# The kernel transform of an S4D convolution: first stage in three float16 products, normalisation and copies on ScalarE

## The chip, the cores and the metric

The kernel runs on one core of a Trainium2 chip. A core has five engines that run their own instruction streams: TensorE (PE, matrix products into PSUM), VectorE (DVE), ScalarE (ACT), GpSimd (POOL) and SyncE (SP, which here only issues transfers). Each engine works through its instructions in order and waits on semaphores of the others. The metric is the device time of one execution in microseconds (us), lower is better; the median of the runs is compared.

## The reference

Four layers are applied one after the other to `x` (2048 positions, 640 channels), each to the layer-normalised `x` and added to it: attention (32 heads of 20), an S4D convolution, the same attention and the same convolution again.

```python
x = x + _A_ref(_layernorm(x), A_wqkv, A_wo)
x = x + _B_ref(_layernorm(x), B_log_A_real, B_A_imag, B_C_real, B_C_imag, B_log_dt, B_D_skip)
x = x + _A_ref(_layernorm(x), A_wqkv, A_wo)
x = x + _B_ref(_layernorm(x), B_log_A_real, ...)

def _B_ref(u, ...):                     # the convolution
    P = jnp.exp((A * dt[:, None])[:, :, None] * pos[None, None, :])
    K = 2.0 * jnp.einsum("dn,dnl->dl", C, P).real        # 640 kernels of length 2048
    Kf = jnp.fft.rfft(K, 2 * L)
    Uf = jnp.fft.rfft(u_t, 2 * L)
    y = jnp.fft.irfft(Uf * Kf[None, :, :], 2 * L)[:, :, :L]
    return y + u * D_skip[None, None, :]
```

The kernels `K` do not depend on `x`, so they and their transforms are computed once and serve both convolutions.

## The kernel before

**The order of the program.** First a prologue: layer norm, the first projections and the tables of powers from which `K` is built (`kgen`). Then attention of the first layer, during which `kgen` makes `K` piece by piece in the gaps of VectorE and TensorE and writes it to `kd` in memory, 32 channels at a time. Then `out_proj` (the attention's output projection), into which `ktransform` is woven; then the convolution `ssm`; then attention, `out_proj` and `ssm` of the second pair, without `kgen` and `ktransform`. A scheduler fixes the order of instructions on each engine when the program is built. In attention a planner with costs of its own decides what goes between two exponentials.

**`out_proj`** runs over 16 slices `s` of the positions (128 each). Per slice it does 30 products of 320 columns: `L1099` with the low part `ol` of the attention's output, `L1105` with its high part `oh`, into two banks `po` of PSUM. VectorE adds `po` to `x` and takes the statistics of the rows (`BN_STATS`, `BN_AGGR`, then `va`, `lt`, `rs`). `ln_u` makes the normalised rows `u` on VectorE, ScalarE rounds them to float16 (`uh`), and GpSimd, or for the last slice VectorE, takes the rest (`ul`). The first convolution needs `uh` and `ul` of all slices. In the first pair the low part `ol` has one buffer, in the second two.

**`ktransform`** runs over five units of 128 channels. A unit
- loads 1 MB of `kd` into `kl` (one buffer) and adds the skip weight to its first column,
- turns it round in 16 transposes `pkt` (`L1054`), four to a bank; VectorE and ScalarE take turns in copying the banks to `ktr`,
- does the first stage, 32 float32 products `pkx` of 128 columns (`L1062`) with the cosine and sine matrix `e1` of 2 MB; the eight banks are copied to `kx` by ScalarE and VectorE in turn,
- goes eight times through `q`: four transposes (`L1071`) into a bank, a copy to `kxt` on ScalarE, a float32 product `pkf` of 512 columns (`L1079`), two shuffles of it to the two halves of `kn` on VectorE, and a sign on one half by ScalarE. Two rounds of `q` fill a pair `kn`, and two transfers of 512 KB write it to `kha` and `khb`. The pair has one buffer.

In the profile a float32 product counts as two matmul records. The tiles `pkt`, `pkx`, `pkf` and `po` have two banks each. The profile shows tile names without their trailing digits; names that then coincide stand with a number in the listings of order below.

**`ssm`** begins with `stage1` (`L1164`): the same transform of the normalised rows, already as three float16 products with a high and a low part of the matrix (`e1s`), twelve products of 128 columns to a bank. ScalarE copies the bank to the high part of `x1`, VectorE takes the low part (both read `x` in the profile: `x<-psx`). `stage2a` (`L1174`) transposes these.

Of the kernel before, what the change touches and what calls it, by code (L numbers as in the profile page):

```python
# [21 lines left out]
P = 128  # L22
L = 2048
D = 640
NI = L // P
NCT = D // P
# [58 lines left out]
def mha_s4d_kernel(ctx, tc, x_in, wqkv, wo, lar, aim, cr, ci, ldt, dsk,  # L85
                   c_e1, c_eb, c_f2, c_fa, c_sel, c_lv, c_id, c_sg, c_e16, c_f16, c_id16, out, parts="asas", general=None):
# [25 lines left out]
    kd = dram.tile([D, L], F32, name="kd")  # L112
# [17 lines left out]
    ve.memset(hpi, math.pi / 2)  # L130
    flag = cp.tile([P, 2], F32, name="flag")
    warm = cp.tile([P, 1], F32, name="warm")
    ve.memset(flag, 0.0)
    with tc.tile_pool(name="op", bufs=1) as op:
        oneh = op.tile([1, L], F16, name="oneh")
# [46 lines left out]
    def kgen():  # L182
# [8 lines left out]
        for n, a in (("lar", lar), ("aim", aim), ("cr", cr), ("ci", ci)):  # L191
            ld[n] = (klp if n in ("lar", "aim") else kp).tile([P, D], F32, name="k_" + n)
            if n in ("lar", "aim"):
                sy.dma_start(ld[n], a)
        dt = klp.tile([P, D], F32, name="k_dt")
        d5 = klp.tile([P, D // P], F32, name="k_d5")
        ge.dma_start(d5, ldt.rearrange("o (p c) -> (o p) c", c=D // P))
# [144 lines left out]
        for r in range(2):  # L342
            ve.memset(tab[:, r, :, 0:24].rearrange("p d (g k) -> p d g k", k=8)[:, :, :, 0:1], 1.0 - r)
        yield from expand(0, kpw[0], tab, dif)
        load_powers(2)
        yield
        for k in range(NE):
# [663 lines left out]
            return oh, ol  # L1011
        return split, lambda: o.append(load(0))

    def ln_u(x, i0, n, mvrs, uh, ul, pool):
        mv, rs = mvrs
        for i in range(n):
            s = i0 + i
            u = pool.tile([P, D], F32, name="u")
            ve.tensor_scalar(u, x[:, s, :], mv[:, i, 0:1], rs[:, i:i + 1], ALU.subtract, ALU.mult)
            se.copy(uh[:, s, :], u)  # L1020
            (ve if s == NI - 1 else ge).tensor_sub(ul[:, s, :], u, uh[:, s, :])  # L1021

# [4 lines left out]
    def by_channel(x1, i2):  # L1027
        return x1[:, :, i2].rearrange("p g (s c) -> p s g c", c=4)

    def ktransform():  # L1030

        c = ExitStack()
        c1 = c.enter_context(tc.tile_pool(name="f1", bufs=1))
        c2 = c.enter_context(tc.tile_pool(name="f2", bufs=2))
        e1 = c1.tile([P, NI, 2, P], F32, name="e1")
        sy.dma_start(e1, c_e1.rearrange("p (i r k) -> p i r k", i=NI, r=2))
        f2 = c1.tile([P, P], F32, name="f2")
        sy.dma_start(f2, c_f2)
        sgn = c1.tile([P, 1], F32, name="sgn")
        sy.dma_start(sgn, c_sg)  # L1040

        skip = c1.tile([P, NCT], F32, name="skip")
        sy.dma_start(skip, dsk)

        def unit_load(b):
            kl = c1.tile([P, L], F32, name="kl")
            sy.dma_start(kl, kd[b * P:b * P + P, :])
            ve.tensor_add(kl[:, 0:1], kl[:, 0:1], skip[:, b:b + 1])
            kt = c1.tile([P, NI, P], F32, name="ktr")
            klv = kl.rearrange("d (p i) -> d i p", i=NI)  # L1050
            for i4 in range(4):
                pt = pst("T", [P, 4, P], F32, tag="T", name="pkt")
                for i in range(4):
                    te.transpose(pt[:, i, :], klv[:, 4 * i4 + i, :], ident)  # L1054
                (se.copy if i4 % 2 else ve.tensor_copy)(kt[:, 4 * i4:4 * i4 + 4, :], pt)
                yield
            x1 = c1.tile([P, 32, NI // 2, 16], F32, name="kx1")
            for i2 in range(NI // 2):
                ps = pst("X", [P, 2, 2, P], F32, tag="X", name="pkx")
                for r in range(2):  # L1060
                    for i in range(2):
                        te.matmul(ps[:, r, i, :], e1[:, 2 * i2 + i, r, :], kt[:, 2 * i2 + i, :],  # L1062
                                  start=True, stop=True)
                (ve.tensor_copy if i2 % 2 else se.copy)(by_channel(x1, i2), ps.rearrange("p r i (g c) -> p (r i) g c", c=4))
                yield
            prev = None
            for q in range(9):
                if q < 8:
                    pt = pst("T", [P, 4, P], F32, tag="T", name="pkt")
                    for g in range(4):  # L1070
                        te.transpose(pt[:, g, :], x1[:, 4 * q + g].rearrange("p i s -> p (i s)"), ident)  # L1071
                    xt = c2.tile([P, 512], F32, name="kxt")
                    se.copy(xt, pt.rearrange("p g k -> p (g k)"))
                if prev is not None:
                    g0 = b * 32 + 4 * (q - 1)
                    if q % 2:
                        kn = [c1.tile([P, 2, 512], F32, name=f"kn{s}") for s in range(2)]
                    px = pst("F", [P, 512], F32, tag="F", name="pkf")
                    te.matmul(px, f2, prev, start=True, stop=True)  # L1079
# [268 lines left out]
    def seq(x, general):  # L1348

        stats = None  # L1350
        for n in range(0, len(parts), 2):
            with ExitStack() as c:
                if general:
                    if stats is not None:
                        xpools.pop().__exit__(None, None, None)
                    attention_general(x)
                else:
                    x, wc, *tail = attention(x, stats)
                psum(c, X=2)
                c3 = ExitStack()  # L1360
                if n == 0 and not general:
                    psum(c3, M=2, T=2, F=2)
                else:
                    psum(c3, M=4)
                up = c.enter_context(tc.tile_pool(name="up", bufs=1))
                uh = up.tile([P, NI, D], F16, name="uh")
                ul = up.tile([P, NI, D], F16, name="ul")
                consts = ssm_consts(c)
                with ExitStack() as c2:
                    up2 = c2.enter_context(tc.tile_pool(name="up2", bufs=2))  # L1370

                    def ln(i0, m):
                        ln_u(x, i0, m, ln_stats(lambda i: x[:, i0 + i, :], m), uh, ul, up2)
                    if general:
                        for i0 in range(0, NI, LG):
                            ln(i0, LG)
                    else:
                        if n == 0:
                            filler[:] = ktransform(), 0.0, False
# [91 lines left out]
```

## Time and profile before

| | us |
|---|---|
| median of 3 runs | 2705.94 |
| lowest and highest | 2704.41, 2708.41 |
| the profiled execution's own time | 2710.14 |
| its span from first to last instruction | 2708.3 |
| TensorE busy in the span | 2532.1 (93%) |
| ScalarE busy | 2336.7 (86%) |
| VectorE busy | 1478.1 (55%) |
| GpSimd busy | 853.2 (32%) |
| `out_proj` of the first pair, first to last of its products | 1104.4 to 1285.5 |

The profile is of one execution. Its rows give a start, a duration and, in brackets, the idle time of the engine just before the instruction and what ended it. Matmuls overlap: a row's duration is the time through the array, and the spacing of starts is what a product costs in a stream. "PEclk" is the TensorE clock that was granted, 1.00 being full speed. The listings of groups give, after the bar, the busy time of all instructions of the group, the mean duration in ns, and the idle time before them with the engine and tile that ended it.

### The profile page before, as it was taken

Reading aid. Unit: us, or ns where it says so; the run is one execution under the profiler, and the core shown is the slowest. Engines: PE = TensorE matmul, PEld = TensorE weight load, DVE = VectorE, ACT = ScalarE, POOL = GpSimd, SP = SyncE. Lnnn points to the kernel's source line nnn. Section 1 sums busy time; section 2 is a strip of 40 time slices with the busy share of each in tenths; the row PEclk is TensorE's granted clock in tenths of the full one; section 3 lists DMA queues with packets and bytes.
Section 4 is the critical chain, followed back from the end, with each engine's and each line's share of the span. In section 5 each row is a group of like instructions: output and inputs, shape, how many; then the busy total and the mean of one; then the engine's idle time right before and its main releaser. Section 6 shows DMA issues by size and latency. Waiting matters only on the chain.

```text
span 2708.3 us, 115632 instructions
## 1 busy us (share of the span) xinstructions
PE 2532.1 (93%) x50944; PEld 1443.4 (53%) x50944; DVE 1478.1 (55%) x3292; ACT 2336.7 (86%) x2762; POOL 853.2 (32%) x1282
## 2 busy tenths in 40 slices
PE   6899999999999998899999999999999998888998
PEld 3445444444444433777896544454454443335888
DVE  7677877777856993567776423232233220003865
ACT  7899989999999999555655899999999999997464
POOL 1132323233332334300671122222223223222376
PEclk9999999999999999999999999999999999999999
DMA  6523222322221224454642111211121112112365
GB/s 205 182 59 78 63 77 57 81 60 70 62 54 49 56 67 140 148 193 189 193 152 67 48 53 50 53 56 46 43 64 41 51 37 60 41 38 81 112 190 162
DMA packets 183152, 238.55 MB, mean 88 GB/s; under 512 B 42736, under 2 KB 128240, under 8 KB 180848
## 3 DMA queue, kind: packets, MB, share of 16 engines
q1 hardware_dynamic: 146304, 184.48, 21.3%
q0 software_dynamic: 36336, 46.59, 7.6%
q8 instruction: 402, 6.59, 1.0%
q14 instruction: 110, 0.90, 0.1%
HBM read 154.90 MB, written 76.03 MB: 85 GB/s over the span
## 4 chain that ended last, share of the span: by engine, by line
ACT 50%; PE 29%; issue 9%; DVE 7%; DMA 4%; POOL 0%; SPq 0%; ACTq 0%; DVEq 0%; POOLq 0%
ACT pt L77 49%; PE pa L842 5%; PE S L825 3%; PE psv L1199 3%; PE po L1105 3%; PE psy L1209 2%; PE m L578 2%; PE psx L1187 2%; PE psx L1164 2%; PE po L1099 1%; PE pst L1174 1%; PE pkf L1079 1%; DMA kop<-ks 1%; PE pq L731 1%; PE pkx L1062 1%
## 5 line engine op out<-in xcount | busy, mean ns | idle before, releaser
L77 ACT ACTIVATE pt<-S 128x1024 f32<-128x1024 f32 x2048 | 1922.5, 1037 | 40.3 <-PE S L825 30.8
L842 PE MATMUL pa<-pt,V 64*32 64x512 f32 x16384 | 1104.2, 591 | 1.0 <-DVE oc L77 0.6
L825 PE MATMUL S<-qop,kop 61*32 61x512 f16 x16384 | 884.7, 381 | 118.0 <-ACT pt L77 102.5
L825 PEld LDWEIGHTS <-kop 61*32 61x32 f16 x16384 | 374.6, 90 | 777.5 <-issue 653.5
L77 POOL DMA_DIRECT2D dn<-oc x256 | 125.7, 497 | 732.9 <-DVE oc L77 696.3
L842 PEld LDWEIGHTS pa<-pt,V 64*32 64x32 f32 x16384 | 316.5, 106 | 72.4 <-issue 8.9
L77 DVE TENSOR_SCALAR qc<-m 128x512 f32<-128x512 f32 (+1 forms) x68 | 46.8, 689 | 313.7 <-PE m L578 313.7
L77 DVE COPY oc<-pa 128x512 f32<-128x512 f32 x64 | 44.2, 690 | 305.3 <-PE pa L842 297.6
L77 POOL DMA_DIRECT2D db<-dn x256 | 129.5, 512 | 131.3 <-DMA dn<-dr 128.0
L578 PE MATMUL m<-xh,wh 64*32 64x512 f16 x2560 | 148.7, 380 | 1.6 <-DVE qc L77 1.6
L578 PE MATMUL m<-xh,wl 64*32 64x512 f16 x2560 | 149.0, 379 | 0.0
L578 PE MATMUL m<-xl,wh 64*32 64x512 f16 x2560 | 146.9, 378 | 0.0
L77 POOL DMA_DIRECT2D ot<-oc x256 | 129.8, 515 | 11.3 <-issue 5.2
L578 PEld LDWEIGHTS <-wh 64*32 64x32 f16 x5120 | 93.1, 94 | 74.8 <-issue 33.0
L1192 POOL TENSOR_TENSOR t<-t,kb 128x512 f32<-128x512 f32 x80 | 101.8, 1273 | 70.7 <-DVE t L77 69.7
L77 ACT COPY xt<-pst 128x1024 f16<-128x1024 f16 x80 | 81.6, 1023 | 46.7 <-PE pst L1174 46.6
L77 POOL DMA_DIRECT2D dn<-dr x64 | 35.7, 558 | 244.9 <-DVE dr L77 235.2
L77 DVE TENSOR_SCALAR V<-m 128x160 f32<-128x160 f32 x64 | 20.7, 324 | 160.0 <-PE m L544 160.0
L77 DVE TENSOR_TENSOR kb<-ktab 128x512 f32<-128x512 f32 x160 | 107.8, 693 | 0.0
L544 PEld LDWEIGHTS <-xh 128*128 128x128 f16 x960 | 79.6, 98 | 48.0 <-issue 32.8
L1021 POOL TENSOR_TENSOR ul<-u,uh 128x640 f16<-128x640 f32 x30 | 46.2, 1557 | 177.1 <-ACT uh L77 177.1
L1193 POOL TENSOR_TENSOR t<-t,t 128x512 f32<-128x512 f32 x78 | 99.1, 1271 | 7.3 <-DVE t L77 1.3
(269 smaller groups left out, 3952.2 us busy)
## 6 DMA issues: line engine op xcount, KB each, us to landing
ka<-kha SPq DMA_DIRECT2D x80, 256.0 KB
kb<-khb SPq DMA_DIRECT2D x80, 256.0 KB
db<-dn POOLq DMA_DIRECT2D x256, 64.0 KB, 2.8
kpw<-wd POOLq DMA_DIRECT2D x60, 192.0 KB, 5.1
qop<-qs SPq DMA_DIRECT2D x256, 40.0 KB
kop<-ks SPq DMA_DIRECT2D x128, 80.0 KB
ot<-oc POOLq DMA_DIRECT2D x256, 40.0 KB, 2.7
otl<-ot SPq DMA_DIRECT2D x32, 320.0 KB
```

The lines of the kernel that those rows point to most:

```text
L77: made = f(out, *a, **k)
L544: chain(te.matmul(ps[:, :n], a_[:, ct, sl], m[:, ct, :], start=(k == 0), stop=(k == 14)))
L578: chain(te.matmul(ps[r][32 * t:32 * t + 32, :], a_[rows, ct, 32 * u:32 * u + 32], m[rows, ct, 512 * v:512 * v + 512], start=(k == 0), stop ...
L825: chain(te.matmul(S[32 * t:32 * t + 32, 512 * r:512 * r + 512], kt_[rows, kc + 32 * t:kc + 32 * t + 32], qt[rows, :], start=True, stop=Tru ...
L842: chain(te.matmul(pa[r][32 * j:32 * j + 32, :], V[rows, kt, VP * h:VP * h + 32], pts[j // 2][rows, 512 * (j % 2):512 * (j % 2) + 512], sta ...
L1105: te.matmul(pos[hf], oh[:, ct, :], m[:, ct, 320 * hf:320 * hf + 320], start=False, stop=(ct == NCT - 1 and m is wol))
L1164: te.matmul(ps[:, r, i, :], e1[:, e, s, r, :], m[:, s, bs], start=(n == 0), stop=(n == 2))
L1187: te.matmul(px, f2[:, f, :], xt[:, k, :], start=(n == 0), stop=(n == 2))
L1192: ge.tensor_mul(t2, t2, kb)
L1193: (ge if g0 else ve).tensor_add(t1, t1, t2)
L1199: te.matmul(pv[:, g].rearrange("p r i c -> p (r i c)"), t1[:, g * P:g * P + P], fa, start=True, stop=True)
L1209: te.matmul(py[:, i, :], eb[:, 4 * i4 + i, r, :], v[:, r, 4 * i4 + i].rearrange("p g c -> p (g c)"), start=(r == 0), stop=(r == 1))
```

## The change

The first stage of `ktransform` is now computed as `stage1` computes it, in three float16 products with `e1s`, which `ssm` has loaded anyway; the float32 matrix `e1` and its load of 2 MB are gone. So that `K` fits float16, it is scaled by a power of two that is found from the largest values of the inputs (`kbig`, `kmost`, `bound`); the scale is undone in the copy to `kxt`.

```diff
+            ve.reduce_max(big[:, n:n + 1], t, axis=AX.X, apply_absolute_value=True)   # three of them, in kgen
+        ge.partition_all_reduce(most, big, P, bass.bass_isa.ReduceOp.max)
+        slow.append((1, bound))                                     # bound(): seven operations on one column
...
-    def ln_u(x, i0, n, mvrs, uh, ul, pool):
+    def ln_u(x, i0, n, mvrs, uh, ul, pool, on_act):
+        if on_act:
+            nb = sm.tile([P, n], F32, name="nb1")
+            ve.scalar_tensor_tensor(nb, mv[:, :, 0], -1.0, rs, ALU.mult, ALU.mult)
...
+            if on_act:
+                se.activation(u, x[:, s, :], AF.Identity, scale=rs[:, i:i + 1], bias=nb[:, i:i + 1])
+            else:
+                ve.tensor_scalar(u, x[:, s, :], mv[:, i, 0:1], rs[:, i:i + 1], ALU.subtract, ALU.mult)
...
-        e1 = c1.tile([P, NI, 2, P], F32, name="e1")
-        sy.dma_start(e1, c_e1.rearrange("p (i r k) -> p i r k", i=NI, r=2))
...
+        def load(b):
+            kl = c2.tile([P, L], F32, name="kl")
+            sy.dma_start(kl, kd[b * P:b * P + P, :])
+            return kl
+        kls = [load(0)]
         def unit_load(b):
-            kl = c1.tile([P, L], F32, name="kl")
-            sy.dma_start(kl, kd[b * P:b * P + P, :])
+            kl = kls.pop()
+            if b + 1 < NCT:
+                kls.append(load(b + 1))
...
-                (se.copy if i4 % 2 else ve.tensor_copy)(kt[:, 4 * i4:4 * i4 + 4, :], pt)
+                se.activation(hi[:, s4, :], pt, AF.Copy, scale=ksc[:, 0:1])
+                ve.scalar_tensor_tensor(lo[:, s4, :], pt, ksc[:, 0:1], hi[:, s4, :], ALU.mult, ALU.subtract)
...
-                for r in range(2):
-                    for i in range(2):
-                        te.matmul(ps[:, r, i, :], e1[:, 2 * i2 + i, r, :], kt[:, 2 * i2 + i, :],
-                                  start=True, stop=True)
-                (ve.tensor_copy if i2 % 2 else se.copy)(by_channel(x1, i2), ...)
+                for i in range(2):
+                    s = 2 * i2 + i
+                    for r in range(2):
+                        for n, (e, m) in enumerate(((0, hi), (0, lo), (1, hi))):
+                            te.matmul(ps[:, r, i, :], e1[:, e, s, r, :], m[:, s, :], start=(n == 0), stop=(n == 2))
+                (ve.tensor_copy if i2 % 4 == 1 else se.copy)(by_channel(x1, i2), ...)
...
-                    se.copy(xt, pt.rearrange("p g k -> p (g k)"))
+                    se.activation(xt, pt.rearrange("p g k -> p (g k)"), AF.Copy, scale=ksc[:, 1:2])
...
-                        kn = [c1.tile([P, 2, 512], F32, name=f"kn{s}") for s in range(2)]
+                        kn = [c2.tile([P, 2, 512], F32, name=f"kn{s}") for s in range(2)]
```

`c1` has one buffer per tile and `c2` two, so `kl` and `kn` now have two. `on_act` holds for the first pair only: there the 16 normalised rows `u` are made by ScalarE.

The scheduler has laid out the surroundings anew, in the prologue, in the first `out_proj` and for a few transfers between; attention keeps its order, and nothing is moved from the first `stage2a` on. Three places matter. In the changed kernel the lines are further down: `L1054` is `L1085`, `L1062` is `L1097`, `L1071` is `L1105` (which before was a line of `out_proj`), `L1079` is `L1113`, and `out_proj`'s two lines are `L1133` and `L1139`.

TensorE in the rounds of `q` of the first unit; before:

```order
L1079 MATMUL pkf<-kxt,f_26611 128x512
L1071 MATMUL pkt<-ident,kx_26645 128x128 x8
L1099 MATMUL po<-woh,ol 128x320 x2
L1071 MATMUL pkt<-ident,kx_26645 128x128 x4
L1105 MATMUL po<-woh,oh 128x320
```

and of the change:

```order
L1113 MATMUL pkf<-kxt,f_26627 128x512
L1105 MATMUL pkt<-ident,kx_26668 128x128 x4
L1085 MATMUL pkt<-ident,kl 128x128 x4
L1133 MATMUL po<-woh,ol 128x320 x3
L1085 MATMUL pkt<-ident,kl 128x128 x2
```

Before, after the fourth `pkf` of a unit, a block of 16 to 20 products of `out_proj` stood ahead of the next `pkf`. Now the first six `pkf` of a unit follow one another with only their transposes between, and the transposes of the next unit begin before the last two. The first transposes of `ktransform` stand behind 184 products of `out_proj` (before: 240 of the 480), and 170 are left when its last `pkf` is through (before: 25).

VectorE at the end of `out_proj`, from the statistics of the last slice; before:

```order
L77 BN_AGGR mv<-st 128x2
L77 TENSOR_SCALAR lt<-lt 128x1
L77 TENSOR_SCALAR va<-mv 128x1
L77 TENSOR_TENSOR rs<-rs,lt 128x1
L77 TENSOR_SCALAR u<-x,mv,rs 128x640
L77 RECIPROCAL rs<-lt 128x1
```

with the first `x_28307<-psx_28308,x_28306` eight rows further, behind the last `ul<-u,uh`; and of the change:

```order
L77 BN_AGGR mv<-st 128x2
L77 TENSOR_SCALAR va<-mv 128x1
L77 TENSOR_TENSOR x_28684<-psx_28685,x_28683 128x4x32x4
L77 RECIPROCAL rs<-lt 128x1
L77 TENSOR_TENSOR lt<-rs 128x1
L77 TENSOR_TENSOR lt<-lt,va 128x1
L77 TENSOR_TENSOR x_28684<-psx_28700,x_28683 128x4x32x4
```

Seven of the first eight low parts of `stage1` now stand ahead of the last `ul`; before, all of them stood behind it.

SyncE's queue near the end of attention, of the change:

```order
L77 DMA wot<-in_wo 128x640 x5
L77 DMA x<-in_x_in 128x2560
L77 DMA kl<-kd 128x2048
L77 DMA qop_107<-qs 40x1x512
L77 DMA qop_107<-qs 20x512
```

The first load of `kl` has come into attention, ahead of the queries `qop` of its last block of 512 (the row `kl` is new there, the others are as before). It waits for the writes of `kd`.

More of the change, by code (lines that the diff above doesn't have):

```diff
@@ L132, in mha_s4d_kernel @@
     warm = cp.tile([P, 1], F32, name="warm")
+    ksc = cp.tile([P, 2], F32, name="ksc")
     ve.memset(flag, 0.0)
@@ L194, in kgen @@
                 sy.dma_start(ld[n], a)
+        big = kp.tile([P, 3], F32, name="kbig")
+        most = kp.tile([P, 3], F32, name="kmost")
+        skip = kp.tile([P, NCT], F32, name="kskip")
+        sy.dma_start(skip, dsk)
         dt = klp.tile([P, D], F32, name="k_dt")
@@ L344, in kgen, with bound @@
         yield from expand(0, kpw[0], tab, dif)
+        for n, t in enumerate((ld["cr"], ld["ci"], skip)):
+            ve.reduce_max(big[:, n:n + 1], t, axis=AX.X, apply_absolute_value=True)
+        ge.partition_all_reduce(most, big, P, bass.bass_isa.ReduceOp.max)
+        def bound():
+            b = big[:, 0:1]
+            bits = b.bitcast(mybir.dt.int32)
+            ve.tensor_add(b, most[:, 0:1], most[:, 1:2])
+            ve.tensor_scalar(b, b, float(P), 1e-30, ALU.mult, ALU.max)
+            ve.tensor_add(b, b, most[:, 2:3])
+            ve.tensor_single_scalar(bits, bits, 0x7F800000, ALU.bitwise_and)
+            ve.reciprocal(ksc[:, 0:1], b)
+            ve.tensor_scalar_mul(ksc[:, 0:1], ksc[:, 0:1], 2.0 ** 14)
+            ve.tensor_scalar_mul(ksc[:, 1:2], b, 2.0 ** -14)
+        slow.append((1, bound))
         load_powers(2)
@@ L1018, in ln_u @@
             u = pool.tile([P, D], F32, name="u")
-            ve.tensor_scalar(u, x[:, s, :], mv[:, i, 0:1], rs[:, i:i + 1], ALU.subtract, ALU.mult)
+            if on_act:
+                se.activation(u, x[:, s, :], AF.Identity, scale=rs[:, i:i + 1], bias=nb[:, i:i + 1])
+            else:
+                ve.tensor_scalar(u, x[:, s, :], mv[:, i, 0:1], rs[:, i:i + 1], ALU.subtract, ALU.mult)
             se.copy(uh[:, s, :], u)
@@ L1028, in by_channel, with ktransform @@
         return x1[:, :, i2].rearrange("p g (s c) -> p s g c", c=4)
-    def ktransform():
+    def ktransform(e1):
         c = ExitStack()
@@ L1043, in ktransform @@
         sy.dma_start(skip, dsk)
+        def load(b):
[3 more added lines that the diff above has]
+        kls = [load(0)]
         def unit_load(b):
-            kl = c1.tile([P, L], F32, name="kl")
-            sy.dma_start(kl, kd[b * P:b * P + P, :])
+            kl = kls.pop()
+            if b + 1 < NCT:
+                kls.append(load(b + 1))
             ve.tensor_add(kl[:, 0:1], kl[:, 0:1], skip[:, b:b + 1])
-            kt = c1.tile([P, NI, P], F32, name="ktr")
+            hi, lo = (c1.tile([P, NI, P], F16, name=f"ktr{n}") for n in "hl")
             klv = kl.rearrange("d (p i) -> d i p", i=NI)
@@ L1054, in unit_load @@
                     te.transpose(pt[:, i, :], klv[:, 4 * i4 + i, :], ident)
-                (se.copy if i4 % 2 else ve.tensor_copy)(kt[:, 4 * i4:4 * i4 + 4, :], pt)
+                s4 = slice(4 * i4, 4 * i4 + 4)
+                se.activation(hi[:, s4, :], pt, AF.Copy, scale=ksc[:, 0:1])
+                ve.scalar_tensor_tensor(lo[:, s4, :], pt, ksc[:, 0:1], hi[:, s4, :], ALU.mult, ALU.subtract)
                 yield
@@ L1059, in unit_load @@
                 ps = pst("X", [P, 2, 2, P], F32, tag="X", name="pkx")
-                for r in range(2):
-                    for i in range(2):
-                        te.matmul(ps[:, r, i, :], e1[:, 2 * i2 + i, r, :], kt[:, 2 * i2 + i, :],
-                                  start=True, stop=True)
-                (ve.tensor_copy if i2 % 2 else se.copy)(by_channel(x1, i2), ps.rearrange("p r i (g c) -> p (r i) g c", c=4))
+                for i in range(2):
[3 more added lines that the diff above has]
+                            te.matmul(ps[:, r, i, :], e1[:, e, s, r, :], m[:, s, :], start=(n == 0), stop=(n == 2))
+                (ve.tensor_copy if i2 % 4 == 1 else se.copy)(by_channel(x1, i2), ps.rearrange("p r i (g c) -> p (r i) g c", c=4))
                 yield
@@ L1372, in ln @@
                     def ln(i0, m):
-                        ln_u(x, i0, m, ln_stats(lambda i: x[:, i0 + i, :], m), uh, ul, up2)
+                        ln_u(x, i0, m, ln_stats(lambda i: x[:, i0 + i, :], m), uh, ul, up2, n == 0 and not general)
                     if general:
@@ L1378, in seq @@
                         if n == 0:
-                            filler[:] = ktransform(), 0.0, False
+                            filler[:] = ktransform(consts[0]), 0.0, False
                         out_proj(x, *tail, ln)
```

## The prediction

> **What bounds the kernel now.** I read busy time by stretch first. Columns: from:to, length, then busy time (and instructions) of PE, PE's weight loads, DVE, ACT, POOL, the granted clock, DMA share and GB/s.
>
> ```profile
> core 0: us, PE busy (x) PEld busy (x) DVE busy (x) ACT busy (x) POOL busy (x), PEclk, DMA share, GB/s
> 130.00:600.00 470.00, 456.60 (x12484) 227.78 (x12479) 367.13 (x758) 453.78 (x483) 147.52 (x252) 1.00 0.27 67
> ...
> 80.00:100.00 20.00, 17.53 (x91) 8.09 (x89) 15.02 (x30) 19.41 (x30) 0.00 (x0) 1.00 0.70 262
> ...
> 1104.00:1294.00 190.00, 179.74 (x1178) 150.49 (x1171) 139.91 (x369) 90.18 (x154) 30.90 (x33) 0.99 0.54 196
> 1290.00:1300.00 10.00, 6.03 (x71) 5.86 (x70) 7.61 (x10) 5.18 (x10) 1.29 (x1) 0.66 0.85 310
> ```
>
> In attention ACT works 453.78 of 470 us: what the change adds there on VectorE and GpSimd has to delay ACT before it costs anything. In the prologue ACT is full too (19.41 of 20). In the first `out_proj`, where the change lies, PE is the full engine: 179.74 of 190 us, against 139.91 on DVE and 90.18 on ACT. So next comes the order of time on PE (start, duration, line, tile, records; in brackets idle time and what ended it).
>
> ```profile
> 1104.37 1.73 PE L1099 MATMUL po<-woh,ol 128*128 128x320 f32 x10
> ...
> 1144.76 1.14 PE L1054 MATMUL pkt<-ident,kl 128*128 128x128 f32 x8 [1.47 <-issue]
> 1146.23 1.17 PE L1054 MATMUL pkt<-ident,kl 128*128 128x128 f32 x8 [0.33 <-DVE ktr L77]
> 1147.23 7.84 PE L1062 MATMUL pkx<-ktr,e 128*128 128x128 f32 x64
> 1154.83 1.13 PE L1099 MATMUL po<-woh,ol 128*128 128x320 f32 x6
> ...
> 1158.65 1.02 PE L1079 MATMUL pkf<-kxt,f 128*128 128x512 f32 x2
> 1159.51 0.60 PE L1071 MATMUL pkt<-ident,kx 128*128 128x128 f32 x4
> 1159.95 1.08 PE L1079 MATMUL pkf<-kxt,f 128*128 128x512 f32 x2
> ...
> 1285.47 0.23 PE L1164 MATMUL psx<-uh,e1s 128*128 128x128 f16 x1
> ...
> 2480.63 1.70 PE L1099 MATMUL po<-woh,ol 128*128 128x320 f32 x10 [1.65 <-DVE oc L77]
> 2550.95 0.31 PE L1105 MATMUL po<-wol,oh 128*128 128x320 f32 x1
> ```
>
> The second pair's `out_proj` has the same 480 products alone: 2480.63 to 2550.95 and one more product, 70.5 us. In the first pair it takes 1104.37 to 1285.47, 181.1 us. Its parts: `out_proj` 70.5; 40 rounds of `q` of 1.30 (1158.65 to 1159.95), 52.0; 80 transposes of 0.125 (eight from 1146.23 to 1147.23), 10.0; five first stages of 7.60 (1147.23 to 1154.83), 38.0. Sum 170.5, so PE loses about 10.6 us to waits. The stage is bound by PE's own work, and work taken from PE is worth its time.
>
> **The change part by part.** *First stage.* The 64 records of a unit (320 in all) cost 7.60/64 = 119 ns each. The 96 float16 products that replace them have the shape, type and matrix of `stage1`; twelve of these, undisturbed, stand between these rows:
>
> ```profile
> 1348.68 0.22 PE L1164 MATMUL psx<-uh,e1s 128*128 128x128 f16 x1
> ...
> 1349.35 1.11 PE L1199 MATMUL psv<-fa,t 128*128 128x128 f32 x8
> ...
> L1164 PEld LDWEIGHTS <-e1s x960: 95/98/148, 1285.5 to 2662.2; 128*128 128x128 f16 x192
> ```
>
> 0.67 us for twelve, 56 ns each; 480 cost 26.8 us instead of 38.0: **-11.2 us**. A weight load takes 98 ns by the third row (minimum/median/maximum), but loads overlap there, since products start every 56 ns. Were this hidden part lost, 480 x 98 = 47.0 us would stand in place of 38.0, a loss of 9.0; these are the two ends, and I take the first, as the rows are of the same instruction. The Trainium skill, "TensorE: Matmul & The Clock Gate", section "Back-to-back issue gap", gives about 81 ns per product of 128 columns for a sustained stream of weight loads and products, and calls some 56 ns the figure of a single gap. By it the stage would cost an estimated 480 x 81 = 38.9 us, and the exchange would gain nothing; this trace has 56 ns in a stream and disagrees.
>
> *Copies around it.* Groups of this stage (busy, mean ns of one):
>
> ```profile
> L77 DVE STREAM_SHUFFLE kn<-pkf 128x512 f32<-128x512 f32 x80 | 54.8, 737 | 0.1
> L77 DVE COPY kx<-pkx 128x512 f32<-128x512 f32 x20 | 13.8, 688 | 8.1 <-PE pkx L1062 8.0
> L77 ACT COPY kx<-pkx 128x512 f32<-128x512 f32 x20 | 11.7, 584 | 17.4 <-PE pkx L1062 17.3
> L77 DVE COPY ktr<-pkt 128x512 f32<-128x512 f32 x10 | 6.8, 683 | 1.2 <-PE pkt L1054 1.2
> L77 DVE TENSOR_SCALAR u<-x,mv,rs 128x640 f32<-128x640 f32 x16 | 11.2, 725 | 0.7
> L77 DVE TENSOR_TENSOR lt<-rs 128x2 f32<-128x2 f32 x7 | 1.1, 155 | 0.1
> ...
> L77 ACT ACTIVATE xr<-xr,nb,rs 128x640 f32<-128x640 f32 x16 | 14.0, 926 | 2.2 <-DVE nb L77 2.0
> ```
>
> DVE loses the 16 `u` (11.2), 10 `ktr` (6.8) and 10 of 20 `kx` (6.9): 24.9 us. It gains 20 low parts `lo`, an operation that the trace does not show; between the shuffle's 0.737 and the `ktr` copy's 0.683 us I take 0.69, the plain copy of the same bank: 13.8 us. With nine `nb` of 0.155 that is -9.7 net: 139.9 falls to 130. ACT gains 10 `hi` and 10 `kx` at 0.584 and 16 `u` at 0.926 (the `xr` row is this very operation): 5.8 + 5.8 + 14.8 = 26.4; 90.2 becomes 117 of some 178 us, still two thirds full. Neither becomes the bound over the stage, so I cost the copies at nothing; PE's work covers them. Locally: twelve products fill a bank in 0.67 us, and two banks are emptied by ACT in 0.584 or DVE in 0.688; with 0.1 us of handover that is (0.67 + 0.69 + 0.1)/2 = 0.73 per bank at worst against 0.67, 40 x 0.06 = 2.4 us if it held throughout.
>
> *Waits inside the stage, and the order.* Wait groups name this one:
>
> ```profile
> DVE kn L77 <- DMA kha<-kn: 8.7, 5, 2.2
> ```
>
> DVE stands 8.7 us, five times, because the single pair `kn` is still being written out; the second pair removes that, and the early load of `kl` the 1.47 us ahead of 1144.76. At the same time the rounds of `q` now follow one another with little `out_proj` between. Each round needs two shuffles, 2 x 0.737 = 1.47 us of DVE, and PE needs 1.30: 40 x 0.17 = 6.8 us lost if DVE did nothing else and PE had nothing to slip in. So the sum of waits, 10.6 before, may fall by 8 or rise by 7. The two have the same size, and I take 0. Also the 2 MB load of `e1` is gone; PE's own rows show no wait for a transfer there but the 1.47, so it is worth nothing.
>
> *The end of the stage.* Between PE's last `po` and the first transposes of `stage2a`:
>
> ```profile
> 1293.91 0.27 PE L1164 MATMUL psx<-uh,e1s 128*128 128x128 f16 x1 [5.04 <-DVE x L77]
> ...
> 1299.34 0.40 PE L1174 MATMUL pst<-id,x 128*128 128x128 f16 x4
> ...
> 1290.01 1.63 DVE L77 TENSOR_SCALAR u<-x,mv,rs 128x640 f32<-128x640 f32 x1
> 1292.43 0.82 DVE L77 TENSOR_TENSOR ul<-u,uh 128x640 f16<-128x640 f32 x1 [0.79 <-ACT uh L77]
> 1293.17 2.48 DVE L77 TENSOR_TENSOR x<-psx,x 128x512 f16<-128x512 f32 x4
> ...
> 2561.68 0.61 PE L1174 MATMUL pst<-id,x 128*128 128x128 f16 x8 [0.37 <-ACT x L77]
> ```
>
> First pair: 1285.47 to 1299.34, 13.9 us. PE waits 5.04 us for a low part `x<-psx` that is queued on DVE behind the last `u` and `ul`, and then runs at a lower clock (0.66 granted in 1290 to 1300). In the second pair, whose `x<-psx` do not stand behind the last `ul`, the same takes 2551.10 to 2561.68, 10.6 us. The new order lets the low parts go ahead as in the second pair: at most -3.3. But the last `u` costs 0.926 + 0.155 on ACT, and ACT also copies `x`: at worst the new chain is 0.9 longer than before. I take **-2.0**.
>
> *Prologue.*
>
> ```profile
> L77 ACT ACT_TABLE_LOAD x18 | 23.1, 1283 | 1.8 <-PEq L1460 0.7 <-PE S L825 0.7
> ```
>
> ACT's new order has one table load more ahead of attention, 1.283 us on a full engine: **+1.3**. The reordering may leave it covered (0) or put up to two more loads' time on the chain (+4).
>
> *Attention.* VectorE takes three reductions and some seven one-column operations (0.155 each), GpSimd one maximum over partitions; all are under ACT's cover, cost 0. The `kl` load now stands in SP's queue ahead of the last `qop`, and waits for the last write of `kd`:
>
> ```profile
> 1041.63 1.10 SPq L77 DMA_DIRECT2D qop<-qs  x2
> ...
> 1047.28 0.25 SPq L77 DMA_DIRECT2D qop<-qm  x1
> ...
> L77 POOL DMA_DIRECT2D kd<-ko x1: 957/957/957, 1047.3 to 1047.3; - x1
> ...
> DMA to landing us min/median/max: 8.6/8.6/8.6
> ...
> 1099.69 0.41 PE L825 MATMUL S<-qop,kop 61*32 61x512 f16 x8 [0.35 <-ACT pt L77]
> ...
> 1101.53 0.41 PE L825 MATMUL S<-qop,kop 61*32 61x512 f16 x8 [0.35 <-ACT pt L77]
> ```
>
> `kd` lands at 1047.3 + 8.6 = 1056; the twelve `qop` loads, which took 5.7 us to issue (1041.63 to 1047.28), then end near 1062. They serve the last 512 columns, 16 pairs of products spaced 1.84 us (1099.69 to 1101.53), so from about 1101.5 - 16 x 1.84 = 1072 on. Some 10 us of margin: cost 0; if a landing took twice as long, PE and then ACT would stall up to 5.
>
> Sum: -11.2 - 2.0 + 1.3 = -11.9. The profiled execution becomes 2710.14 - 11.9 = 2698.2; it lies 4.2 above the median of the runs, so the median becomes 2705.94 - 11.9 = **2694.0**, faster by 0.44%.
>
> **The rivals.** *Denser:* the second `kn` pair, the early `kl` and a DVE with 10 us less work take out most of PE's waits. For it: 8.7 of DVE's idle time has this one cause. Against it: PE mostly had `out_proj` products to run meanwhile. 2694.0 - 7 = 2687. *Given back:* the packed rounds of `q` run at DVE's pace. For it: 1.47 over 1.30, and `lo` falls to the same engine. Against it: the next unit's first stage and `out_proj` fill gaps. 2694.0 + 6.8 = 2700.8. *Weight loads not hidden (slower):* each of the new first stages switches matrix and operand within one stream, and if loads did not overlap there, 98 ns would set the pace: 2705.94 + 9.0 - 2.0 + 1.3 = 2714.2. It decides from 79 ns per product (38.0/480) on. Against it stand the 56 ns of `stage1`, which switches in the same way. It is also the side on which the 81 ns of the Trainium skill lie. *Cover gone:* the load of `kl` blocks SP's queue beyond 1072, and the prologue costs its +4: 2694.0 + 5 + 2.7 = 2701.7. That the change does less than it says is excluded for the main term: 96 products a unit and no load of `e1` stand in the new order.
>
> **How the numbers follow.** Forecast 0.56, denser 0.14, given back 0.16, weight loads 0.08, cover gone 0.06. About 0.2%, 5.4 us, is what a measurement of this kernel can tell from no change: faster means below 2700.5. That holds the forecast (its own range is 2688 to 2701), denser, and the smaller part of given back: 0.73. Same: the rest of given back and most of cover gone, with a rim of the forecast, 0.17. Slower: the weight loads and some of the last, 0.10. The range 2685 to 2706 leaves out about 0.05 below and 0.12 above.
>
> **What would show it.** Right: the new `pkx` rows start every 56 ns, 5.4 us per unit; first `po` to first `psx` takes about 170 us; the last `po` to the first `pst` takes 11 to 12; no PE wait above 1 us for `qop` near 1072. Given back shows as PE's waits for DVE `kn` ahead of `pkf`, 7 us or more; denser as a stage of 162 us or less with no DVE wait for `kha`; the weight loads as `pkx` spacings near 98 ns. The forecast is wrong if the stage's work falls by 11 us while its length falls by less than 5.

## The result, and the profile after

| | before | after |
|---|---|---|
| median, us | 2705.94 (5 runs, 2704.41 to 2708.41) | 2693.66 (5 runs, 2692.22 to 2694.99) |
| ratio to before | | 0.9954, 95% interval [0.9939, 0.9968] |
| own time of the profiled execution | 2710.14 | 2693.68 |
| attention's first exponential | 116.75 | 115.36 |
| first `po` to first `psx` (the stage) | 181.1 | 170.6 |
| from the product behind the last `po` to first `pst` (its end) | 13.9 | 11.3 |
| first `po` to first `pst` | 195.0 | 181.9 |

The change gains 12.3 us; 11.9 were forecast. The two profiled executions differ by 16.5 us, since that of before lies 4.2 above its median; 13.1 of the 16.5 are in the last line of the table, which is therefore the line to follow.

First the busy time by stretch, for the changed kernel (columns as in the prediction):

```profile
core 0: us, PE busy (x) PEld busy (x) DVE busy (x) ACT busy (x) POOL busy (x), PEclk, DMA share, GB/s
80.00:100.00 20.00, 17.59 (x89) 7.92 (x87) 14.97 (x31) 17.76 (x29) 0.12 (x1) 0.98 0.67 247
130.00:600.00 470.00, 455.44 (x12482) 229.11 (x12489) 372.97 (x777) 453.22 (x483) 148.75 (x254) 1.00 0.26 67
1102.00:1292.00 190.00, 182.20 (x1484) 150.74 (x1479) 143.53 (x378) 126.22 (x202) 34.23 (x35) 1.00 0.52 188
1273.00:1284.00 11.00, 8.09 (x127) 7.22 (x126) 10.21 (x24) 8.10 (x15) 2.06 (x2) 1.00 0.47 145
...
1102.00:1273.00 171.00, 167.74 (x1288) 138.75 (x1283) 127.57 (x346) 113.07 (x181) 29.68 (x32) 1.00 0.50 184
```

Attention is as it was. In the stage itself (the last row) PE is busy 167.74 of 171 us, DVE 127.57, ACT 113.07: PE is still the full engine. At the end (1273 to 1284) the granted clock is 1.00, where 0.66 was granted in 1290 to 1300 before.

The order of time on PE for the changed kernel, from the first `po` over one run of the new first stage to the first `pst`:

```profile
1102.33 1.73 PE L1133 MATMUL po<-woh,ol 128*128 128x320 f32 x10
...
1141.20 0.22 PE L1097 MATMUL pkx<-ktrh,e1s 128*128 128x128 f16 x1
...
1142.48 0.22 PE L1097 MATMUL pkx<-ktrh,e1s 128*128 128x128 f16 x1
...
1272.92 0.23 PE L1198 MATMUL psx<-uh,e1s 128*128 128x128 f16 x1
...
1278.70 0.22 PE L1198 MATMUL psx<-uh,e1s 128*128 128x128 f16 x1 [1.36 <-DVE lt L77]
...
1284.18 0.62 PE L1208 MATMUL pst<-id,x 128*128 128x128 f16 x8
```

Between 1141.20 and 1142.48 stand 24 products, that is 23 spacings of 55.7 ns. At the end no wait is longer than 1.36 us, where there was one of 5.04.

What the prediction did not look at is when `ktransform` is through. Here are its last writes to `khb` on SP's queue (issue times), before

```profile
1281.31 0.32 SPq L77 DMA_DIRECT2D khb<-kn  x1
...
1287.66 0.32 SPq L77 DMA_DIRECT2D khb<-kn  x1
```

and after:

```profile
1247.53 0.32 SPq L77 DMA_DIRECT2D khb<-kn  x1
...
1250.39 0.32 SPq L77 DMA_DIRECT2D khb<-kn  x1
```

Before, the last pair left 2.3 us after the last `po` (1285.32); now it leaves 22 us ahead of it (1272.77). The experiments show that the second buffer of `kn`, with which the transform ends this early, is needed for the gain as much as PE's lighter work is.

### The profile page after: what moved, and what is told of

It is laid out like the page before. It is cut to its first block, busy times and chain, and to the rows that moved or that the text cites. A ratio compares the mean times of both kernels' runs of the same rounds, so it can differ in the third digit from the quotient of the medians.

```text
span 2691.8 us, 116010 instructions
## 1 busy us (share of the span) xinstructions
PE 2519.0 (94%) x51104; PEld 1432.0 (53%) x51104; DVE 1473.7 (55%) x3295; ACT 2364.3 (88%) x2799; POOL 855.2 (32%) x1283
## 4 chain that ended last, share of the span: by engine, by line
ACT 50%; PE 27%; issue 9%; DVE 6%; DMA 3%; SPq 1%; POOL 0%; ACTq 0%; DVEq 0%; POOLq 0%
ACT pt L77 49%; PE pa L862 4%; PE psv L1233 3%; PE psy L1243 3%; PE S L845 3%; PE po L1139 2%; PE psx L1221 2%; PE m L598 2%; PE psx L1198 1%; PE po L1133 1%; PE pkf L1113 1%; PE pst L1208 1%; DVE ktab L77 1%; DMA qop<-qs 1%; PE pq L751 1%
## 5 line engine op out<-in xcount | busy, mean ns | idle before, releaser
L1227 POOL TENSOR_TENSOR t<-t,t 128x512 f32<-128x512 f32 x78 | 99.3, 1273 | 8.6 <-DVE t L77 2.6
L320 PEld LDWEIGHTS m<-kb,ka 128*32 128x32 f32 x3840 | 61.0, 109 | 72.0 <-issue 56.1
```

Source lines behind the costliest of these rows:

```text
L320: chain(te.matmul(ps[32 * j:32 * j + 32, c8, :], a[n][:, ch, :], b[n][:, dd, :], start=(n == 0), stop=(n == 2), tile_position=(0, 32 * j)))
L1227: (ge if g0 else ve).tensor_add(t1, t1, t2)
```

## The experiments

The ratio of each is to the kernel before on the same chip (medians there 2707.0 to 2707.2). The changed kernel was measured beside a before of 2705.94, so differences of medians between it and the experiments are good to about 1 us. "Window" is first `po` to first `pst`, "end" is from the product behind the last `po` to the first `pst`, "last khb" the time from the first `po` to the last issue of a write to `khb`, all in us and of the one execution in each run's trace, which lies up to 4.2 us off the median (before +4.2, e8 +4.0, e11 +3.9). In e4, e5, e10 and e11, 12 to 24 products of `stage1` (56 ns each) already stand ahead of the last `po`, in e8 five and in e6 and e9 one, so the window is the safer measure. Where "the stage" is named for a run, it ends with the last `po`.

| run | median us | ratio to before, interval | window | end | last khb |
|---|---|---|---|---|---|
| before | 2705.94 | | 195.0 | 13.9 | 183.3 |
| after | 2693.66 | 0.9954 [0.9939, 0.9968] | 181.9 | 11.3 | 148.1 |
| e1 float32 again, one buffer | 2710.89 | 1.0016 [1.0007, 1.0025] | 198.8 | 15.7 | 188.4 |
| e2 one buffer | 2702.77 | 0.9988 [0.9979, 0.9997] | 192.6 | 22.4 | 181.9 |
| e3 float16 alone | 2707.06 | 0.9998 [0.9989, 1.0007] | 195.7 | 23.0 | 185.6 |
| e4 `u` on VectorE | 2695.33 | 0.9958 [0.9944, 0.9972] | 183.1 | 10.8 | 145.7 |
| e5 one `kn` | 2702.66 | 0.9987 [0.9978, 0.9995] | 188.9 | 15.2 | 176.3 |
| e6 one `kl` | 2693.06 | 0.9954 [0.9941, 0.9967] | 182.3 | 11.3 | 152.4 |
| e7 float16, half pairs | 2694.14 | 0.9954 [0.9941, 0.9967] | 183.9 | 11.4 | 165.5 |
| e8 float32, half pairs | 2707.58 | 1.0000 [0.9991, 1.0009] | 195.8 | 10.9 | 170.8 |
| e9 products twice | 2718.65 | 1.0042 [1.0028, 1.0057] | 208.2 | 11.3 | 165.6 |
| e10 second stage float16 | 2711.21 | 1.0015 [1.0006, 1.0023] | 197.9 | 13.9 | 166.3 |
| e11 the same, `kx` on ScalarE | 2710.28 | 1.0012 [1.0004, 1.0021] | 200.0 | 12.5 | 165.9 |

**e1: the first stage back in float32.** Of the changed kernel:

```diff
-            hi, lo = (c1.tile([P, NI, P], F16, name=f"ktr{n}") for n in "hl")
+            kt = c1.tile([P, NI, P], F32, name="ktr")
...
-                            te.matmul(ps[:, r, i, :], e1[:, e, s, r, :], m[:, s, :], start=(n == 0), stop=(n == 2))
+                        te.matmul(ps[:, r, i, :], e1[:, 2 * i2 + i, r, :], kt[:, 2 * i2 + i, :], start=True, stop=True)
...
-            kl = c2.tile([P, L], F32, name="kl")          # and kn
+            kl = c1.tile([P, L], F32, name="kl")
```

> The changed kernel with its first stage of the kernels' transform back in float32 (320 records with e1, loaded again); since e1 takes the room, kl and kn have one buffer each; the rows u stay on ScalarE, three of four kx copies too. If the gain is PE's work (prediction): the five first stages take 7.6 us each again, first po to first psx grows from 170.6 to 181 or more, time 2705 +- 3, that is 11 us above the run with one buffer and float16. If the gain came from the rows on ScalarE or the copies: 2697 or less.

2710.89, above the 2705 +- 3 that I had put down and even 0.16% slower than before: the rows and copies on ScalarE bring nothing by themselves with the float32 stage. Against e2, which differs only in the first stage and the copies ahead of it, it is 8.1 us slower, not 11.2.

**e2: one buffer for `kl` and `kn`.** The last two lines of e1's diff alone, and no load ahead.

> The changed kernel with one buffer each for kl and kn, and no early load of kl. Prediction (waits inside the stage worth 0): 2694 to 2697, first po to first psx 170 to 173. Rival denser (the second buffers carry several us): 2700 or more, with DVE waiting 8 us for kha again and PE waiting for it.

2702.77: the rival, and 9 us worse than the changed kernel. But not by waits inside the stage, which is as short as after (170.2): the end has grown to 22.4 us, in which ScalarE's first `x<-psx` waits 3.35 us for a write to `khb`.

**e3: the float16 first stage alone.** As e2, and

```diff
-                (ve.tensor_copy if i2 % 4 == 1 else se.copy)(by_channel(x1, i2), ...)
+                (ve.tensor_copy if i2 % 2 else se.copy)(by_channel(x1, i2), ...)
...
-    ... up2, n == 0 and not general)
+    ... up2, False)
```

> The kernel before with the float16 first stage and its scale alone: rows u on VectorE, kx copies alternating, one buffer for kl and kn. Prediction: -11.2 on PE stays, the end of the stage (last po to first pst) goes back to 13 to 14 us: 2696 to 2698. Rival (the other parts are needed because VectorE, which now has 13.8 us of lo more and nothing less but ktr, becomes the bound): 2700 or more.

2707.06, no gain at all, where I had expected some 9 us. (e2, which differs only in `u` and a part of the `kx` copies on ScalarE, is 4.3 us faster; their intervals overlap at the rim. With one buffer these may help; with two they are not needed, as e7 shows.) The stage lost its 8.3 us (172.8 against 181.1), and the end gave back 9.1. This is how, in the order of time of e3 on three engines and SP's queue:

```profile
1278.99 0.16 DVE L77 TENSOR_TENSOR lt<-rs 128x1 f32<-128x1 f32 x1
1281.58 0.01 DVE L77 LOAD_MASK_SELECT kn<-pkf  x1 [2.43 <-DMA kha<-kn]
...
1282.85 0.14 DVE L77 TENSOR_TENSOR lt<-lt,va 128x1 f32<-128x1 f32 x1
...
1286.27 0.72 DVE L77 STREAM_SHUFFLE kn<-pkf 128x512 f32<-128x512 f32 x1
...
1286.44 1.33 ACT L77 ACTIVATE kn<-kn,sgn 128x512 f32<-128x512 f32 x2 [1.59 <-DVE kn L77]
...
1287.80 0.32 SPq L77 DMA_DIRECT2D khb<-kn  x1
...
1290.58 2.05 ACT L77 CAST x<-psx 128x512 f16<-128x512 f32 x4 [2.81 <-DMA khb<-kn]
...
1291.20 1.29 DVE L77 TENSOR_TENSOR x<-psx,x 128x512 f16<-128x512 f32 x2 [4.21 <-ACT x L77]
...
1291.95 0.29 PE L1195 MATMUL psx<-uh,e1s 128*128 128x128 f16 x1 [12.01 <-DVE x L77]
```

Read it from below. PE stands 12.01 us for a low part `x<-psx`. VectorE makes it only after ScalarE's `x<-psx`, and that waits for a transfer with which it has no data in common, the last write of `kn` to `khb`: the tile `x` of the convolution lies in the room that `ktransform` gives up, so the room must be read out first. That write was late because the last shuffle (1286.27) stood on VectorE behind a wait of 2.43 us for the write of the pair before, in the same single buffer, and behind the last slice's statistics (`lt`), `u` and `ul`, which this wait had delayed too. The pairs followed one another in some 6 us:

```profile
1246.79 0.32 SPq L77 DMA_DIRECT2D khb<-kn  x1
...
1253.09 0.32 SPq L77 DMA_DIRECT2D khb<-kn  x1
...
1258.93 0.32 SPq L77 DMA_DIRECT2D khb<-kn  x1
```

With two buffers the pairs of a unit follow in some 3 us (1247.53, 1250.39 above). Not all of this is waiting. The scheduler lays out another order when `kn` has one buffer: in e3, as before, blocks of `out_proj` products stand between the rounds of `q`, and all 480 stand ahead of the last `pkf` (455 before, 310 after, 458 in e5, which differs from the changed kernel in the buffer of `kn` alone). No run keeps the order and changes only the buffer, so what the waits alone cost stays open. The last write to `khb` goes at 1287.80 here and at 1287.66 before: PE had been relieved of 11 us, and the transform ended no earlier.

**e4: `u` back on VectorE.** The last two lines of e3's diff.

> The changed kernel with the rows u of the first out_proj back on VectorE (+11.2 us there, -14.3 on ScalarE). Prediction: first po to first psx stays at 170 to 172, last po to first pst goes from 11.3 back to 13 to 14: +2 to +3, 2696. Rival given back (VectorE is close to setting the pace): stage 175 or more, 2700 or more. Rival (the tail has nothing to do with u): 2694.

2695.33, with an interval that overlaps that of the change almost whole; the window is 183.1 against 181.9 and the end no longer than after. My reason for the shorter end falls: the place where `u` is made doesn't decide it.

**e5 and e6: one `kn`, or one `kl`.** From here on the theory is that of e3.

```diff
-                        kn = [c2.tile([P, 2, 512], F32, name=f"kn{s}") for s in range(2)]      # e5
+                        kn = [c1.tile([P, 2, 512], F32, name=f"kn{s}") for s in range(2)]
```

```diff
-            kl = c2.tile([P, L], F32, name="kl")                                               # e6
+            kl = c1.tile([P, L], F32, name="kl")
...
-        kls = [load(0)]
```

> The changed kernel with one buffer for the pair kn; kl keeps two and its early load. Theory now (with one kn the transform ends after the last po, its last write to khb holds the memory that the first x<-psx takes, and PE waits for that): last khb issue after 1275, last po to first pst 17 us or more, time 2699 to 2703. Rival (kl is what matters): 2694 to 2696.

> The changed kernel with one buffer for kl and no early load; kn keeps two. Theory: the transform starts some 3 us later but its rounds run freely, so it still ends long before the last po: last po to first pst 11 to 12, time 2693 to 2696. Rival (kl matters): 2699 or more.

2702.66 and 2693.06: it is `kn`. The second `kl` and its load ahead are worth nothing measurable. In e5 the end is 15.2 us, below the 17 that I had put down, while the stage is 3.1 longer than after (173.7). Nor is it the way that the theory names. These are the rows of e5 on VectorE and PE:

```profile
1282.12 1.49 DVE L77 TENSOR_TENSOR ul<-u,uh 128x640 f16<-128x640 f32 x1 [3.03 <-ACT uh L77]
1283.54 2.47 DVE L77 TENSOR_TENSOR x<-psx,x 128x512 f16<-128x512 f32 x4
...
1284.27 0.27 PE L1198 MATMUL psx<-uh,e1s 128*128 128x128 f16 x1 [6.31 <-DVE x L77]
```

PE's wait of 6.31 us leads to the last `ul`, behind which all low parts `x<-psx` are queued, as in the kernel before; no engine is seen to wait for `khb` there. Over all thirteen kernels the order on VectorE goes with the buffer: in the five with one `kn` (before, e1, e2, e3, e5) no low part stands ahead of the last `ul`, in the eight with two 7 to 10 do.

**e7 and e8: half pairs.** The same remedy in no more memory, on e3 and on the kernel before:

```diff
-                    if q % 2:
-                        kn = [c1.tile([P, 2, 512], F32, name=f"kn{s}") for s in range(2)]
+                    kn = [c2.tile([P, 512], F32, name=f"kn{s}") for s in range(2)]
...
-                    if q % 2 == 0:
-                        for s, dst in enumerate((kha, khb)):
-                            sy.dma_start(dst[:, g0 - 4:g0 + 4, :].rearrange("p g k -> p (g k)"), ...)
+                    for s, dst in enumerate((kha, khb)):
+                        sy.dma_start(dst[:, g0:g0 + 4, :].rearrange("p g k -> p (g k)"), kn[s])
```

> The float16 first stage alone (rows u on VectorE, kx copies alternating, one kl), but with half pairs kn: each round of q has a tile of half the size, two buffers, and its own two writes of 256 KB. No more memory than before. Theory (the wait for kn's writes is what gave the gain back): 2694 to 2699 instead of the 2707 of the float16 stage alone, last po to first pst below 16. Rival (VectorE's own work gave it back, 24 us more than in the changed kernel): 2704 or more.

> The kernel before, only with the half pairs kn in two buffers. Theory (PE's float32 work bounds the stage of 181 us, the buffers only free the end): the stage keeps 178 to 181, last po to first pst falls from 13.9 to 11 to 12; 2702 to 2706. Rival (the buffers alone are the gain): 2697 or less.

e7 reaches 2694.14, the whole gain of the change, without `u` on ScalarE, without the new share of the `kx` copies and without a second `kl`. e8 gets nothing, 2707.58, and misses its range: its end is short (10.9) and its last `khb` early, but the stage itself takes 184.8 us with its float32 products, 3.7 more than before. By the traces PE is busy 178.1 us of it against 176.3 and idle 6.9 against 4.8, its longest waits being for VectorE (`kx`, 1.8; `x<-x,po`, 1.7); why the changed order brings them wasn't followed. So the four cells are: float32 with one buffer 2707, float16 with one 2707, float32 with two 2708, float16 with two 2694. Each half alone is worth nothing, both together 13 us.

**e9: every float16 product of the first stage twice.**

```diff
-                        for n, (e, m) in enumerate(((0, hi), (0, lo), (1, hi))):
-                            te.matmul(ps[:, r, i, :], e1[:, e, s, r, :], m[:, s, :], start=(n == 0), stop=(n == 2))
+                        for n, (e, m) in enumerate(((0, hi), (0, lo), (1, hi)) * 2):
+                            te.matmul(ps[:, r, i, :], e1[:, e, s, r, :], m[:, s, :], start=(n % 3 == 0), stop=(n % 3 == 2))
```

> The changed kernel with each of the 480 float16 products of the first stage done twice (960; the second group of three overwrites the first). Theory (56 ns a product, and PE is what bounds the stage once kn has two buffers): +26.8 us of PE work, time +20 to +27, 2714 to 2721. Rival (PE has room there, the buffers are the gain): +10 at most, below 2704. If weight loads set the pace: +47, 2740.

2718.65, 25.0 us above the changed kernel (23.8 when each is taken against the kernel before on its own chip; the window 26.3), for 480 products more: 50 to 55 ns each. With two buffers in `kn`, PE's work is worth its time.

**e10 and e11: the second stage in float16 too.** The high and low part of `kxt` and three products `pkf` in place of one; the scale goes into the copies `v<-psv`. e11 has every `kx` copy on ScalarE as well.

```diff
-                    se.activation(xt, pt.rearrange("p g k -> p (g k)"), AF.Copy, scale=ksc[:, 1:2])
+                    se.activation(xt[0], ptf, AF.Copy, scale=2.0 ** -5)
+                    ve.scalar_tensor_tensor(xt[1], ptf, 2.0 ** -5, xt[0], ALU.mult, ALU.subtract)
...
-                    te.matmul(px, f2, prev, start=True, stop=True)
+                    for n, (f, k) in enumerate(((0, 0), (0, 1), (1, 0))):
+                        te.matmul(px, f2s[:, f, :], prev[k], start=(n == 0), stop=(n == 2))
```

> The changed kernel with the second stage of the transform in three float16 products too (the high part of kxt by ScalarE, the low part by VectorE; the scale is undone in the later copies v<-psv of the convolution). A float32 pkf takes 0.86 us, three float16 products of 512 columns 0.64: -8.8 us of PE; VectorE gets 40 x 0.69 = 27.6 us more, 155 of some 170. If PE still bounds: 2685 to 2690. If VectorE takes over as the bound: 2694 to 2705.

> As the run before, with all kx copies on ScalarE (-6.9 us on VectorE, +5.8 on ScalarE). If VectorE bounds the run before, this one is 2 to 7 us faster than it; if PE does, they are the same within 2 us.

2711.21 and 2710.28, 17 us slower than the change and above both ranges of e10. PE's waits in e10, the longest three:

```profile
PE pkt L1083 <- DVE ktrl L77: 8.4, 4, 2.2
PE po L1134 <- DVE x L77: 3.3, 3, 2.3
PE psx L1199 <- DVE x L77: 3.1, 4, 2.0
```

and the group that was added:

```profile
L77 DVE SCALAR_TENSOR_TENSOR kxtl<-pkt,kxth 128x512 f16<-128x512 f32 x40 | 26.7, 677 | 6.1 <-ACT kxth L77 6.1
```

PE now waits for VectorE in many places, also for `po`; in the stage it is idle 17.9 us, where the changed kernel has 3.3. That does not make VectorE a full engine: it is busy 153.31 of 188 us (1102 to 1290). And e11, made to test this, speaks against it: with 6.9 us of copies taken off VectorE the time falls by 0.9, no difference that can be told, which was to be the sign of PE as the bound; PE's idle time in the stage is again 17.9 us and its wait for `ktrl` 8.8. So what is shown is that particular results of VectorE come late, `ktrl` first of all, and not that its total of work is the bound. The granted clock in the stage was 0.98 in e10 and 0.96 in e11, against 1.00 in the changed kernel, which is a part of the loss. What sets the pace of both stays open.

## Why the prediction was right, and where it was not

- **First stage on PE, -11.2 us: right in its size.** 480 products at 55.7 ns are 26.7 us, 26.8 were forecast; the doubling agrees. Weight loads stay hidden in this stream: one takes 98 ns (e9), and products start every 55.7. The 81 ns that the Trainium skill ("TensorE: Matmul & The Clock Gate", "Back-to-back issue gap") gives for such a stream would have made an estimated 12 us more; neither these rows nor e9 agree with it.
- **"The stage is bound by PE's own work, and work taken from PE is worth its time": the step that failed as a general statement.** It holds with two buffers in `kn` (e9) and not with one (e3). Beside PE stood a second chain nearly as long, the pairs of `kn`: shuffle, sign, write, wait, with the `out_proj` products that the scheduler puts between them. Before, its last write was issued 2.3 us after PE's last `po`, so it hid behind PE's work, and only just. The 10.6 us of PE "lost to waits" were a remainder of the sum, too: the trace of before has PE idle for 4.8 us of the stage.
- **Waits inside the stage, taken as 0: the sum is right, the price of the buffer is wrong.** The stage fell by 10.5 us where -11.2 was forecast, and DVE's wait for `kha` did go. But I priced the second `kn` only by what it saves inside the stage (up to 8, set against slower rounds). It is worth 9.0 us (e5 against after; 9.6 against e6 on the same chip). In the traces 3.1 us of it lie inside the stage and 3.9 behind the last `po`, which the forecast never connected with the buffer. The 1.47 us that it gave to the load of `kl` are marked `issue` in their row, so no transfer is shown there, and e6 gives the second `kl` nothing.
- **The end, -2.0: -2.6 measured; half of the cause was named.** The order on VectorE that I had named, low parts ahead of the last `ul`, goes with a short end: 10.8 to 11.4 us in the changed kernel, e4 and e6 to e9, which have it, 12.5 and 13.9 in e11 and e10, which have it too, and 13.9 to 23.0 in the five that don't. The place of `u` doesn't matter (e4 10.8 and e7 11.4, with `u` on VectorE). What I had not seen is that this order comes and goes with the second `kn`, and that a late last `khb` can cost more on top: ScalarE's first `x<-psx` waits for it in e2 (3.35 us) and e3 (2.81), not in before or e5 (in e1 it waits 3.1 us for the load `ka<-kha`). That the room given up is what connects the two is read from these two waits; a run with `kn` in a room of its own wasn't tried. Whether the scheduler holds the low parts back for the same reason wasn't tested.
- **Prologue, +1.3: not seen.** The table load is there, and attention starts earlier:

```profile
L77 ACT ACT_TABLE_LOAD x19 | 24.4, 1283 | 5.5 <-issue 3.8 <-PE S L845 0.8 <-PEq L1494 0.7
...
7.55 0.17 DVE L77 TENSOR_SCALAR ee_z<-k_d 128x5 f32<-128x5 f32 x1 [2.19 <-DMA k_d<-in_ldt]
```

  In the profile of before this instruction stood at 9.21, because `k_d`, which GpSimd issues at 2.48 in both, landed later. Over the kernels with 19 table loads attention's first exponential comes between 113.9 and 116.3 us, and at 114.8 in e8, which has 18: 1.3 us can't be told there.
- **Attention, 0: right.** The `qop` loads were held up behind `kl`, the last one to 1058.23, and no product waited for them:

```profile
1048.94 0.33 SPq L77 DMA_DIRECT2D kl<-kd  x1
...
1058.23 0.27 SPq L77 DMA_DIRECT2D qop<-qm  x1
```

- **Rivals.** Denser named the right buffer, but as a bonus of 7 us on top of the forecast; without it 4.4 us of the gain are left (e5), or nothing (e3). Given back did not come: the stage fell short of the 11.2 us by 0.7 only.

So the time was right, to 0.3 us, by luck: two errors met. The relief of PE was priced as if nothing else were near, and the buffer that made this true was priced at 0.

## What to carry to other kernels

When work is taken from the full engine, look for the chain that ends next, and follow it to its last write and to the memory that this write holds: in e2 and e3 a transfer out of a tile decided when the next stage could store its first tile in the same room. Then see what the scheduler makes of a buffer, as it may move more than the wait that the buffer removes. A change that lightens the bound engine and loosens a buffer has to be priced as a pair; undoing one half at a time, in all four cells, shows it, while either half alone would have been thrown away as useless. A buffer of half the size, twice, did as much as a second whole one.

## What the runs showed of the hardware

**A scale from memory.** A copy that takes its scale from a column of memory is longer than the plain one. In the stage of the changed kernel (before, without a scale: 581 ns for `kxt`, 584 for the bank `ktr`):

```profile
L77 ACT ACTIVATE kxt<-pkt,ksc 128x512 f32<-128x512 f32 x40 | 26.5, 676 | 8.8 <-PE pkt L1105 8.8
L77 DVE SCALAR_TENSOR_TENSOR ktrl<-pkt,ksc,ktrh 128x512 f16<-128x512 f32 x20 | 14.4, 743 | 2.3 <-ACT ktrh L77 2.0
...
L77 ACT ACTIVATE ktrh<-pkt,ksc 128x512 f16<-128x512 f32 x20 | 13.2, 684 | 7.9 <-PE pkt L1085 7.9
```

On ScalarE that is 95 to 100 ns, on 60 copies 5.8 us, which the forecast had not counted; no run prices it alone. It is the column and not the scale: in e10 the same copy with a constant as its scale (`kxth`) took 596 ns. On VectorE the low part with a constant as its scale took 677 ns (`kxtl` above), with a column 743; 690 were forecast.

**The clock after a wait.** Between the last `po` and the first `pst` the granted clock was 0.70 to 0.78 in the five kernels with one `kn`, where PE stood 5.0 (before), 7.6 (e1), 11.8 (e2), 12.0 (e3) and 6.3 us (e5) in one piece. It was 1.00 in the changed kernel, e4, e6 to e9 and e11, where the longest wait was 1.0 to 1.6 us, and 0.88 in e10, where it was 2.0 and the clock had been below 1.00 in the stage already. So a long wait at the end cost twice: the rows of e5 above continue with products of `stage1` every 106 ns, where they start every 56 ns otherwise.
